# The first units of a scan in front of an FFN: dummies out, two steps moved, one load split

## The chip, the cores and the metric

One core of one Trainium2 chip runs the program. The time is device microseconds of one execution, and the median of several runs is compared. The engines are TensorE (PE, with its weight loads PEld), VectorE (DVE), ScalarE (ACT), GpSimd (POOL) and SyncE (SP), which only issues DMAs; ScalarE issues one DMA too. Each engine takes its own instructions in the order in which they are written, and waits at an instruction for what that one needs.

## The reference

Two parts. The first is a chunked scan with decays, for 4 batches, 8 heads, 768 steps, head size 32 and state size 16:

```python
log_a = np.log(np.clip(a, 1e-06, 1.0))
for c in range(nc):                       # chunks of the sequence
    cum = np.cumsum(la, axis=-1)
    L = np.exp(cum[:, :, :, None] - cum[:, :, None, :]) * causal
    M = np.einsum('bhin,bhjn->bhij', Cc, Bc) * L
    y_intra = np.einsum('bhij,bhjd->bhid', M, xc)
    y_inter = np.einsum('bhin,bhnd->bhid', Cc, state) * np.exp(cum)[:, :, :, None]
    y[:, :, sl] = y_intra + y_inter
    Bx = np.einsum('bhjn,bhjd->bhjnd', Bc, xc) * np.exp(cum[:, :, -1:] - cum)[:, :, :, None, None]
    state = np.exp(np.sum(la, axis=-1))[:, :, None, None] * state + np.sum(Bx, axis=2)
```

The second is an FFN over the 3072 tokens of 256 channels that the scan gives: `h = x @ w_in` (256 to 2048), `g = max(0.01 * h, h)`, `g @ w_out` (2048 to 256). The FFN weights come as 64-bit floats and are turned into pairs of 32-bit floats on the chip.

## The kernel before

The scan uses chunks of 96 steps instead of 32: 8 chunks times 4 batches are 32 units, and a unit holds the 8 heads of one batch and chunk. For each unit the kernel needs four things.

- **Decays**: the exponent of every pair of steps, made by TensorE into a two-bank buffer `pd`, and an exponential by ScalarE into the tile `lt` (decay_of, L276). Units 0 and 1 do it directly from `la` (decay_mask L239, decay_direct L246). Later units take one product of two tiles `dl` and `dr` (decay_pe, L265). Parts of these hold the running sums, which VectorE splits in three (split_sums, L227 to L230), SyncE writes to DRAM (`parts_d`, L618), and DMAs read back into `dl` (L254) and `dr` (L257). For the first two of these slots the DMA of `dr` is issued by ScalarE.
- **Scores**: products of C and B in two halves (L321), each half in a score buffer of its own; VectorE multiplies them into `lt` (L326).
- **Products**: `lt` with x (L348), and the decayed B with x for the state (L357), into a `pd` buffer.
- **Outputs** (unit_halves): ScalarE copies the state part (`stage`, L381) and rounds the output (`xh`, L386), GpSimd writes the state into the next chunk's x (L384), and `rest()` takes on VectorE what the rounding lost (`xl`, L391).

The decayed B is made once per chunk: the column product (columns, L217) on TensorE, an exponential `erev` on ScalarE (L218), a multiplication on GpSimd (state_decay, L303).

The order is written out by hand: what is called first stands first on every engine that it uses. Two pools of buffers tie the engines together. `ps_c` has two score buffers (score_tile): `first`, with the row sums, and `second`, with the column product in its first bank, are the two at the start, and the two halves of unit 0's scores take the same two again. `ps_d` has two buffers too (free_tile): units 0 and 1's decays take one each, then they alternate, so that the products of a unit take one and the decays of the unit two ahead the other. In the loop over the first ten units the decays of unit u + 2, the scores of unit u + 1 and the products of unit u follow each other; for u = 0 the products come first, so that unit 2's decays take the buffer of unit 1's, and unit 3's decays the buffer of unit 0's products.

keep_warm (L128) issues dummy products on a zero tile, whose results nobody reads: six at the start, two behind the decay masks, two in unit 0 and one ahead of the scores of units 2, 3 and 4. Weight blocks (`raw`, 512 KB each, fetch_w at L100) are decoded by ScalarE (L445) and VectorE (L452 to L472) among the units. Behind the ten units the FFN runs in 54 and more steps on TensorE, with the remaining units between them.

Of the kernel before, what the change touches and what calls it, by code (L numbers as in the profile page):

```python
# [10 lines left out]
F32 = mybir.dt.float32  # L11
# [7 lines left out]
Q = 96  # L19
# [41 lines left out]
BUSY = (17, 21, 25, 30, 34, 38, 42, 46, 50)  # L61
LIGHT = (9, 11, 13, 14, 16)
KD = Q + 3 * NH + 3
MAG_MIN = float(np.uint32(0x38000000).view(np.float32))
MAG_MAX = float(np.uint32(0x47EFFFFF).view(np.float32))

# [2 lines left out]
def scan_ffn(ctx: ExitStack, tc: tile.TileContext, a_l, b_l, c_l, bn_l, x_l, w_l, out_l):  # L69
# [25 lines left out]

    raws, bcs, xss, bns = {}, {}, {}, {}

    def fetch_w(f, eng=nc.sync):
        raws[f] = wr.tile([128, 2 * DM, 2], U32, name="raw")
        eng.dma_start(raws[f].rearrange("p c w -> p (c w)"), w_l[f].bitcast(U32))  # L100

    ccs = [pst.tile([128, 2, NB, Q], F32, name=f"cc{i}") for i in range(2)]

# [22 lines left out]
    def keep_warm(space, n):  # L126
        for _ in range(n):
            nc.tensor.matmul(  # L128
                space.rearrange("p (a b) -> p a b", b=128), lhsT=idle,
                rhs=idle.unsqueeze(1).to_broadcast([128, 4, 128]), start=True, stop=True,  # L130
            )
# [50 lines left out]
    def fill_first():  # L182
        nc.vector.tensor_copy(dr[:Q, 0], later.unsqueeze(1).to_broadcast([Q, NH, Q]))

    def fill_less():
        rows = slice(Q, Q + 3 * NH)
        nc.scalar.copy(dr[rows, 0], less[rows].unsqueeze(2).to_broadcast([3 * NH, NH, Q]))
# [15 lines left out]
        )  # L203

    nc.vector.tensor_copy(upto_b, upto)

    erev = const.tile([QE, ncols], F32, name="erev")
    ccol = const.tile([QE, ncols], F32, name="ccol")
# [100 lines left out]

    def scores(u, warm=0):
        c, b = divmod(u, NB)
        lt = lts[u].rearrange("p (g h) i -> p g (h i)", h=2)
        for half in range(2):
            sc = score_tile()
            if half == 0 and warm:
                keep_warm(sc[:, 0], warm)
            for g in range(2):
                r = 32 * (2 * half + g)  # L320
                nc.tensor.matmul(  # L321
                    sc[:QE, g, :2 * Q].rearrange("p (k i) -> p k i", k=2), lhsT=bcs[c][r:r + 32, b * QE:(b + 1) * QE],
                    rhs=ccs[c % 2][r:r + 32, :, b], start=True, stop=True,
                )
            heads = lt[:, 2 * half:2 * half + 2]
            nc.vector.tensor_tensor(out=heads, in0=sc[:QE, :, :2 * Q], in1=heads, op=ALU.mult)  # L326
# [270 lines left out]
    with tc.tile_pool(name="ps_d", bufs=2, space=PSUM, reuse_waits="tile") as ps_d:  # L597
# [9 lines left out]
        second = score_tile()  # L607
        for u in range(DIRECT):
            fill_reach(u)
        nc.gpsimd.memset(ccs[1], 0.0)  # L610
        nc.vector.memset(dl[Q:], 1.0)
        nc.vector.memset(dl[Q:Q + 3 * NH, :, Q:], 0.0)
        fill_first()
        fill_less()
        prow = first[:, 0, :Q]
        sum_rows(prow, 0)
        split_sums(prow)
        nc.sync.dma_start(parts_d, parts)  # L618
        fetch_w(0)
        for u in range(DIRECT):  # L620
            decay_mask(pds[u])
        keep_warm(second[:, 1], WARM2)
        columns(erev, after, AF.Exp, second[:, 0])
        state_decay(0)
        decay_direct(0, pds[0])
        decay_of(0, pds[0])
        fill_slots(1, SLOTS // 2)
        scores(0)
        decay_direct(1, pds[1])
        nc.scalar.copy(dl[:Q], upto_b.unsqueeze(1).to_broadcast([Q, SLOTS, QE]))  # L630
        decay_load(DIRECT, 2, nc.scalar)
        decay_load(DIRECT + 2, SLOTS - 2)
        decay_of(1, pds[1])
        fill_slots(SLOTS // 2, SLOTS)
# [3 lines left out]
        for u in range(FIRST_UNITS):  # L638
            v = u + 2
            if u:  # L640
                decay_pe(v, free_tile())
            if u == 0:
                rest = unit_out(u, free_tile())
                rest()
            if u + 1 < FIRST_UNITS:
                scores(u + 1, int(0 < u < 4))
            else:
                pair_now((), (u + 1, u + 2))
                settle()
                state_decay(3)  # L650
                abs_more()
                pg = ctx.enter_context(tc.tile_pool(name="pg", bufs=LAG + 2))
                ffn_in(0, free_tile()[:, 0])
            if u:
                rest = unit_out(u, free_tile())
                rest()
            else:
                pd = free_tile()
                keep_warm(pd[:, 0], WARM2)
                decay_pe(v, pd)  # L660
            c, b = divmod(u, NB)
            if u == 1:
                fetch_w(1)
            if c + 2 <= 3:
                if b == 2:
                    fetch_bc(c + 2)
                if b == 3:
                    fetch_bn(c + 2)
            if u == 3:
                fetch_x(2)  # L670
            if u == 5:
                fetch_w(2)
            if u == 7:
                alloc_x(3)
                fetch_x(3)
            if u > 7:
                fetch_more()
            if u in (2, 5):
                state_decay(1 if u == 2 else 2)
            if u:  # L680
                settle()
            if u == 1:
                decode_abs(0)
            if u == 4:
                decode_abs(1)
            decode(LEAD.get(u, 0))
# [326 lines left out]
```

## Time and profile before

| | |
|---|---|
| median of 3 runs | 318.17 us (317.96 to 318.62) |
| profiled execution | 318.41 us, its span 316.7 us |
| busy: PE, DVE, ACT, POOL | 310.4, 212.0, 180.7, 128.5 us |
| first FFN product | at 29.24 us |
| median time of the 512 KB weight loads, issue to landing | 3.3 us |

Times in rows are microseconds from the start of the span. A row of the timeline gives start, length, engine, line, operation, what is written from what, how many instructions were merged, and in brackets how long the engine was idle before and what ended that. PE's lengths reach to the end of the pipeline, so that rows of PE overlap; the distance from one start to the next is what an instruction takes of its queue. A q behind an engine's name is its queue, which issues DMAs.

### The profile page before, as it was taken

What the parts mean: (1) busy time and instruction counts of PE and PEld (TensorE: products, weight loads), DVE (VectorE), ACT (ScalarE), POOL (GpSimd) and SP (SyncE); (2) the same over time, 40 slices, a digit from 0 to 9 for tenths busy, and PEclk for the clock granted to TensorE, in tenths of its full rate; (3) what the DMA queues carried; (4) which work ended last, traced back from release to release, by engine and by line L of the source; (5) the groups of instructions that cost most, each with busy time, mean ns of one, the idle gap of its engine ahead of it and who ended that gap; (6) DMA issues with size and microseconds to landing.
All of it is one profiled execution on the core that took longest, in us unless ns stands there. A gap on an engine that the chain in (4) does not pass through costs nothing.

```text
span 316.7 us, 6261 instructions
## 1 busy us (share of the span) xinstructions
PE 310.4 (98%) x2407; PEld 245.8 (78%) x2407; DVE 212.0 (67%) x350; ACT 180.7 (57%) x353; POOL 128.5 (41%) x215
## 2 busy tenths in 40 slices
PE   8999999999999999999999999999999999999995
PEld 4566877777888878888887878788887888888884
DVE  5697787898987677767634444277367676767561
ACT  3776776848574755646454634375365547645551
POOL 6288644614554242724434330070035466335100
PEclk9999999999999999999999999999999999999999
DMA  6987626094518322350204101000001000000003
GB/s 166 253 223 232 173 81 214 23 274 133 155 67 248 108 89 66 96 126 2 90 0 156 66 1 68 0 2 0 0 0 66 2 0 0 2 0 0 2 2 132
DMA packets 11722, 26.29 MB, mean 83 GB/s; under 512 B 2380, under 2 KB 4652, under 8 KB 11692
## 3 DMA queue, kind: packets, MB, share of 16 engines
q1 hardware_dynamic: 11641, 25.88, 27.3%
q8 instruction: 19, 0.31, 0.4%
q14 instruction: 11, 0.09, 0.1%
q10 hardware_dynamic: 51, 0.01, 0.0%
HBM read 22.57 MB, written 3.32 MB: 82 GB/s over the span
## 4 chain that ended last, share of the span: by engine, by line
PE 95%; DVE 2%; ACT 1%; issue 1%; DVEq 0%; ACTq 0%
PE op L578 27%; PE hp L554 26%; PE sc L800 9%; PE op L820 7%; PE sc L820 6%; PE hp L800 3%; PE sc L411 3%; PE sc L348 3%; PE sc L321 2%; PE pd L348 1%; PE pd L265 1%; PE sc L128 1%; PE pd L246 1%; DVE w L465 1%; PE sc L357 1%
## 5 line engine op out<-in xcount | busy, mean ns | idle before, releaser
L567 DVE TENSOR_TENSOR gl<-hp,gh 128x512 fp32r<-128x512 f32 x63 | 43.4, 689 | 55.4 <-ACT hp L564 55.3
L561 ACT ACTIVATE gh<-hp 128x512 fp32r<-128x512 f32 x63 | 37.6, 598 | 63.0 <-PE hp L554 62.9
L578 PE MATMUL op<-gh,wh 128*128 128x512 f32 x128 | 50.9, 398 | 0.0
L554 PE MATMUL hp<-xh,wh 128*128 128x512 f32 x126 | 50.0, 397 | 0.4 <-DVE gl L567 0.4
L578 PE MATMUL op<-gh,wl 128*128 128x512 f32 x128 | 49.9, 390 | 0.0
L578 PE MATMUL op<-gl,wh 128*128 128x512 f32 x128 | 49.8, 389 | 0.0
L554 PE MATMUL hp<-xl,wh 128*128 128x512 f32 x126 | 49.2, 390 | 0.0
L554 PE MATMUL hp<-xh,wl 128*128 128x512 f32 x126 | 49.2, 390 | 0.0
L384 POOL COPY xs<-stage 16x64 f32<-16x64 f32 x112 | 30.8, 275 | 30.5 <-ACT stage L381 25.9
L766 POOL TENSOR_TENSOR sl<-s,sh 128x512 fp32r<-128x512 f32 x8 | 10.4, 1295 | 71.3 <-ACT sh L765 71.3
L564 ACT ACTIVATE hp<-hp 128x512 f32<-128x512 f32 x63 | 37.5, 595 | 0.0
L297 POOL TENSOR_SCALAR_AFFINE_SELECT lt<-lt 96x768 f32<-96x768 f32 x16 | 15.7, 982 | 47.8 <-ACT lt L296 47.8
L288 POOL TENSOR_TENSOR lt<-lt,ccol 112x768 f32<-112x768 f32 x16 | 25.2, 1577 | 10.8 <-DMA lt<-crow_d 6.0
L578 PEld LDWEIGHTS op<-gh,wh 128*128 128x128 f32 x128 | 24.0, 188 | 7.0 <-issue 1.4
L554 PEld LDWEIGHTS hp<-xh,wh 128*128 128x128 f32 x126 | 23.7, 188 | 5.9 <-DVE gl L567 0.8
L578 PEld LDWEIGHTS op<-gl,wh 128*128 128x128 f32 x128 | 24.0, 188 | 5.1
L554 PEld LDWEIGHTS hp<-xl,wh 128*128 128x128 f32 x126 | 23.6, 188 | 5.4 <-DVE xl L391 0.5
L578 PEld LDWEIGHTS op<-gh,wl 128*128 128x128 f32 x128 | 24.0, 188 | 4.6
L554 PEld LDWEIGHTS hp<-xh,wl 128*128 128x128 f32 x126 | 23.7, 188 | 4.8 <-DVE wl L485 0.2
L424 DVE TENSOR_TENSOR lt<-sc,lt 112x384 f32<-112x384 f32 x44 | 21.6, 548 | 3.5 <-ACT xh L386 1.8
L833 DVE TENSOR_TENSOR gl<-c,gh 128x512 fp32r<-128x512 f32 x24 | 23.1, 962 | 1.0 <-ACT c L830 0.7
L829 ACT ACTIVATE gh<-hp 128x512 fp32r<-128x512 f32 x8 | 4.8, 600 | 27.2 <-PE hp L800 27.2
(164 smaller groups left out, 617.0 us busy)
## 6 DMA issues: line engine op xcount, KB each, us to landing
raw<-w_l SPq DMA_DIRECT2D x16, 512.0 KB, 3.3
lt<-crow_d SPq DMA_DIRECT2D x16, 336.0 KB, 4.6
xs<-x_l SPq DMA_DIRECT2D x8, 384.0 KB, 8.2
out_l<-ob SPq DMA_DIRECT2D x12, 256.0 KB, 2.2
bn<-bn_l SPq DMA_DIRECT2D x8, 231.0 KB, 3.8
bt<-b_l SPq DMA_DIRECT2D x8, 224.0 KB, 6.4
cc<-c_l SPq DMA_DIRECT2D x16, 96.0 KB, 4.6
la<-a_l SPq DMA_DIRECT2D x1, 96.0 KB
```

Of the source, the lines that this page charges most:

```text
L288: nc.gpsimd.tensor_tensor(out=lts[u], in0=lts[u], in1=ccol[:, u * NH:(u + 1) * NH].unsqueeze(2).to_broadcast([QE, NH, Q]), op=ALU.subtract,)
L297: nc.gpsimd.affine_select(out=lt[:Q], in_=lt[:Q], pattern=[[0, NH], [1, Q]], compare_op=ALU.is_ge, fill=0.0, base=0, channel_multiplier=-1,)
L384: nc.gpsimd.tensor_copy(to[:, :, hh], stage[hh * D:hh * D + N])
L424: nc.vector.tensor_tensor(out=heads, in0=spaces[half][:QE, :, 2 * Q * e:2 * Q * (e + 1)], in1=heads, op=ALU.mult,)
L554: nc.tensor.matmul(hp, lhsT=w_half[half][:, f, k * 128:(k + 1) * 128], rhs=x[t][:, k, :], start=(n == 0), stop=(n == 5),)
L561: nc.scalar.activation(ghs[s], hp, AF.Prelu, alpha=0.01)
L564: nc.scalar.activation(hps[s], hps[s], AF.Prelu, alpha=0.01)
L567: nc.vector.tensor_tensor(out=gls[s], in0=hps.pop(s), in1=ghs[s], op=ALU.subtract)
L578: nc.tensor.matmul(op, lhsT=w_half[half][:, f, DM + m * 128:DM + (m + 1) * 128], rhs=x, start=(first and i == 0), stop=(last and i == 2),)
L800: nc.tensor.matmul(bank, lhsT=w[h], rhs=x[g], start=start and i == 0, stop=i == 2, skip_group_check=True,)
L820: nc.tensor.matmul(outs[t][m], lhsT=w_half[half][:, f, DM + m * 128:DM + (m + 1) * 128], rhs=x, start=first and i == 0, stop=last and i == 2,)
L833: nc.vector.tensor_tensor(out=gl, in0=g, in1=gh, op=ALU.subtract)
```

## The change

Seven edits, all ahead of the FFN:

- The dummies of the units go: the two in unit 0, and the one ahead of the scores of units 2, 3 and 4. Those at the start and behind the masks stay.
- The column product, `erev` and the multiplication of B go behind unit 0's direct decays and their exponential.
- The ones in `dl` are set on VectorE ahead of the clipping of `la`, as 32-bit words that hold two ones each.
- ScalarE fills `dl` right behind fill_less, and issues its DMA of `dr` ahead of unit 0's exponential.
- The memset of the second `cc` buffer on GpSimd goes behind the multiplication of B.
- Weight block 0 is loaded in two halves; between them stands the first DMA of `dl`.
- In unit 0, `rest()` goes behind the scores of unit 1.

```diff
-    def fetch_w(f, eng=nc.sync):
-        raws[f] = wr.tile([128, 2 * DM, 2], U32, name="raw")
-        eng.dma_start(raws[f].rearrange("p c w -> p (c w)"), w_l[f].bitcast(U32))
+    def fetch_w(f, half=None):
+        if f not in raws:
+            raws[f] = wr.tile([128, 2 * DM, 2], U32, name="raw")
+        part = slice(0, 2 * DM) if half is None else slice(half * DM, (half + 1) * DM)
+        nc.sync.dma_start(
+            raws[f][:, part].rearrange("p c w -> p (c w)"),
+            w_l[f].bitcast(U32).rearrange("p (c w) -> p c w", w=2)[:, part].rearrange(
+                "p c w -> p (c w)"
+            ),
+        )
...
     nc.vector.tensor_copy(upto_b, upto)
+    nc.vector.memset(dl[Q:].rearrange("p b j -> p (b j)").bitcast(F32), ONES)
...
-    def scores(u, warm=0):
+    def scores(u):
...
             sc = score_tile()
-            if half == 0 and warm:
-                keep_warm(sc[:, 0], warm)
...
             fill_reach(u)
-        nc.gpsimd.memset(ccs[1], 0.0)
-        nc.vector.memset(dl[Q:], 1.0)
+        fill_first()
         nc.vector.memset(dl[Q:Q + 3 * NH, :, Q:], 0.0)
-        fill_first()
         fill_less()
+        nc.scalar.copy(dl[:Q], upto_b.unsqueeze(1).to_broadcast([Q, SLOTS, QE]))
         prow = first[:, 0, :Q]
         sum_rows(prow, 0)
         split_sums(prow)
         nc.sync.dma_start(parts_d, parts)
-        fetch_w(0)
+        fetch_w(0, 0)
         for u in range(DIRECT):
             decay_mask(pds[u])
         keep_warm(second[:, 1], WARM2)
+        fill_slots(1, SLOTS // 2)
+        decay_direct(0, pds[0])
+        decay_load(DIRECT, 2, nc.scalar)
+        decay_of(0, pds[0])
         columns(erev, after, AF.Exp, second[:, 0])
         state_decay(0)
-        decay_direct(0, pds[0])
-        decay_of(0, pds[0])
-        fill_slots(1, SLOTS // 2)
+        nc.gpsimd.memset(ccs[1], 0.0)
         scores(0)
         decay_direct(1, pds[1])
-        nc.scalar.copy(dl[:Q], upto_b.unsqueeze(1).to_broadcast([Q, SLOTS, QE]))
-        decay_load(DIRECT, 2, nc.scalar)
+        fetch_w(0, 1)
         decay_load(DIRECT + 2, SLOTS - 2)
...
             if u == 0:
                 rest = unit_out(u, free_tile())
-                rest()
             if u + 1 < FIRST_UNITS:
-                scores(u + 1, int(0 < u < 4))
+                scores(u + 1)
...
-                pd = free_tile()
-                keep_warm(pd[:, 0], WARM2)
-                decay_pe(v, pd)
+                rest()
+                decay_pe(v, free_tile())
```

How the instructions stand is shown here at three places; line numbers of the changed program are five to nine higher for the same line.

First ScalarE, from the fill of `dr` to unit 1's exponential; `lt` from `pd` is the exponential of a unit's decays, `erev` that of the column product. Before:

```order
L187 COPY dr<-less 24x768
L218 ACTIVATE erev<-sc 112x256
L276 ACTIVATE lt<-pd 112x768
L630 COPY dl<-upto_b 96x896
L257 DMA dr<-parts_d 3x16x96
L276 ACTIVATE lt<-pd 112x768
```

Changed:

```order
L195 COPY dr<-less 24x768
L620 COPY dl<-upto_b 96x896
L266 DMA dr<-parts_d 3x16x96
L285 ACTIVATE lt<-pd 112x768
L227 ACTIVATE erev<-sc 112x256
L285 ACTIVATE lt<-pd 112x768
```

The copy and the DMA moved ahead of unit 0's exponential, and `erev` moved behind it.

Then TensorE, from the column product (`sc` from `la` and `after`) to unit 2's and 3's decays (`pd` from `dr` and `dl`). Before:

```order
L217 MATMUL sc<-la,after 112x256
L246 MATMUL pd<-lt,after 112x384 x2
L321 MATMUL sc<-cc_95,bt 112x192 x4
L246 MATMUL pd<-lt,after 112x384 x2
L348 MATMUL pd<-lt,xs 32x96 x8
L357 MATMUL pd<-xs,bn 32x32 x8
L321 MATMUL sc<-cc_95,bt 112x192 x4
L128 LDWEIGHTS idle
L128 MATMUL pd<-idle 128x512
L128 LDWEIGHTS idle
L128 MATMUL pd<-idle 128x512
L265 LDWEIGHTS dl
```

Changed:

```order
L255 MATMUL pd<-lt,after 112x384 x2
L226 MATMUL sc<-la,after 112x256
L328 MATMUL sc<-cc_95,bt 112x192 x4
L255 MATMUL pd<-lt,after 112x384 x2
L355 MATMUL pd<-lt,xs 32x96 x8
L364 MATMUL pd<-xs,bn 32x32 x8
L328 MATMUL sc<-cc_95,bt 112x192 x4
L274 LDWEIGHTS dl
```

The column product now stands between unit 0's decays and unit 0's scores, and the dummies are gone.

Last VectorE, from the fill of the first `dr` slots to the multiplications of unit 2. Before:

```order
L191 COPY dr<-dr 120x2304
L326 TENSOR_TENSOR lt<-sc,lt 112x384 x2
L191 COPY dr<-dr 120x3072
L391 TENSOR_TENSOR xl<-pd,xh 128x2x96
L326 TENSOR_TENSOR lt<-sc,lt 112x384 x4
```

Changed:

```order
L199 COPY dr<-dr 120x2304
L333 TENSOR_TENSOR lt<-sc,lt 112x384 x2
L199 COPY dr<-dr 120x3072
L333 TENSOR_TENSOR lt<-sc,lt 112x384 x2
L398 TENSOR_TENSOR xl<-pd,xh 128x2x96
L333 TENSOR_TENSOR lt<-sc,lt 112x384 x2
```

The two multiplications of unit 1 now stand ahead of `xl` of unit 0.

More of the change, by code (lines that the diff above doesn't have):

```diff
@@ L63 @@
 KD = Q + 3 * NH + 3
+ONES = float(np.uint32(0x3F803F80).view(np.float32))
 MAG_MIN = float(np.uint32(0x38000000).view(np.float32))
```

## The prediction

> **What bounds the kernel now.** I read the page first, then the chain of waits, then each engine's timeline from 3 to 20 us, where every edit lies.
>
> ```profile
> span 316.7 us, 6261 instructions
> PE 95%; DVE 2%; ACT 1%; issue 1%; DVEq 0%; ACTq 0%
> 11.24 0.54 PE pd L128 x2
> 12.47 0.22 PE sc L128
> 14.31 0.22 PE sc L128
> 16.15 0.22 PE sc L128
> ```
>
> The chain is TensorE's in 95% of the span, and the five dummies that the change takes out of the units lie on it with 0.54 + 3 x 0.22 = 1.20 us. Read no further and that is the gain. But a chain that follows a pipelined engine says little of what that engine waits for, so the stretch itself decides.
>
> ```profile
> 16.00:20.00 4.00, 4.00 (x88) 2.40 (x86) 3.96 (x10) 2.62 (x8) 3.56 (x9) 1.00 0.77 207
> 20.00:24.00 4.00, 3.95 (x89) 2.70 (x88) 3.96 (x12) 3.72 (x11) 3.50 (x10) 1.00 0.85 232
> ```
>
> In these rows of the windows (stretch, length, then busy time of PE, PEld, DVE, ACT and POOL) VectorE has 3.96 of 4.00 us. From 16 us on a unit cannot go faster than VectorE lets it, whatever TensorE saves. Only what moves VectorE's work of unit 3 (L326 at 15.15) reaches the end, and it reaches it whole: behind the units TensorE runs the FFN without slack.
>
> **The column product goes behind unit 0's decays.** Unit 0 now, with every engine that takes part:
>
> ```profile
> 3.34 0.81 DVE L611 MEMSET dl<- 32x896 bf16 x1 [0.24 <-issue]
> 3.69 0.71 PE L221 MATMUL sc<-upto,la 96*128 96x96 f32 x2
> 4.37 0.36 DVE L183 COPY dr<-later 96x768 bf16<-96x768 bf16 x1
> 4.64 0.25 DVE L227 CAST parts<-sc 128x96 bf16<-128x96 f32 x1
> ...
> 6.24 0.60 PE L217 MATMUL sc<-la,after 96*112 96x256 f32 x2
> 6.68 1.45 PE L246 MATMUL pd<-lt,after 96*112 96x384 f32 x4
> 6.88 0.38 ACT L218 ACTIVATE erev<-sc 112x256 f32<-112x256 f32 x1 [2.47 <-PE sc L217]
> 7.34 1.06 POOL L303 TENSOR_TENSOR bn<-bn,erev 112x512 f32<-112x512 f32 x1 [1.15 <-ACT erev L218]
> 7.78 0.75 SPq L254 DMA_DIRECT2D dl<-parts_d  x2
> 8.06 0.59 PE L321 MATMUL sc<-cc,bt 32*112 32x192 f32 x8
> 8.16 0.81 ACT L276 ACTIVATE lt<-pd 112x768 f32<-112x768 f32 x1 [0.91 <-PE pd L246]
> 8.23 0.51 ACTq L257 DMA_DIRECT2D dr<-parts_d  x1
> 8.58 1.54 PE L246 MATMUL pd<-lt,after 96*112 96x384 f32 x4
> ...
> SPq L254 <- DMA parts_d<-parts: 1.0, 1, 1.0
> ```
>
> TensorE runs column product, unit 0's decays, unit 0's scores and unit 1's decays back to back. With the two first exchanged, the decays start at 6.24 instead of 6.68 and end at 6.24 + 1.45 = 7.69; the scores still come at 8.06. The exponential lt of unit 0 could start at 7.72 instead of 8.16, a gain of 0.44.
>
> On ScalarE, though, the DMA of dr now stands ahead of that exponential, and it needs parts_d in DRAM. Today it stands behind it and its wait costs nothing. The memset of 0.81 leaves VectorE's way, so the cast L227 waits only for the row sums (3.69 + 0.71 = 4.40, say 4.45 instead of 4.64), and everything up to parts_d comes 0.2 sooner: landed at about 7.78 - 0.2 = 7.6. The last row, of the waits, shows what such a wait does: SyncE's queue stands still 1.0 us at L254 for parts_d, the DMAs behind it too. ScalarE's will do the same, and issuing takes 0.51, so lt starts at 8.1. The gain of 0.44 shrinks to 0.05.
>
> The Trainium skill ("DMA: Bandwidth & Descriptors", Anatomy of one DMA) says that a semaphore wait of a DMA is taken by the issuing sequencer before dispatch; by that lt stands still until 8.1. By the row at 8.23 alone, an issue beside a running exponential, lt might pass at 7.72, and the stall below would be 0.4 shorter.
>
> Then the price. The column product is written into the second score buffer. There are two such buffers, and the second half of unit 0's scores takes that one again, so it must wait until the exponential erev (L218) has read it. Today erev is done at 7.26, 0.8 before. In the new order erev stands behind lt on ScalarE: from the next two rows ScalarE goes from one lt to the next instruction in 10.87 - 10.16 = 0.71.
>
> ```profile
> 10.06 0.54 PE L348 MATMUL pd<-lt,xs 96*32 96x96 f32 x16
> 10.16 0.81 ACT L276 ACTIVATE lt<-pd 112x768 f32<-112x768 f32 x1 [0.23 <-PE pd L246]
> 10.65 0.59 PE L321 MATMUL sc<-cc,bt 32*112 32x192 f32 x8
> 10.87 0.20 ACT L381 COPY stage<-pd 128x64 f32<-128x64 f32 x1
> ```
>
> So erev runs 8.1 + 0.71 = 8.81 to 9.19, and the second half of the scores starts at 9.25. Scores take 8.58 - 8.06 = 0.52 of TensorE's queue, a half 0.26, and unit 1's decays, queued behind, start at 9.51 instead of 8.58: **+0.93**. TensorE has nothing else: all of unit 0's products stand behind them. Bounds: if the DMA wait does not hold ScalarE, lt at 7.72 gives +0.55; if parts_d comes no sooner, 7.78 + 0.51 gives lt at 8.29 and +1.12. I take 0.93, since a waiting DMA held its queue in the row of L254.
>
> From those decays to the products is 8.06 - 6.68 = 1.38 where nothing intervenes; today it is 10.06 - 8.58 = 1.48, as the products also wait for VectorE. So products at 10.89, **-0.10** of the stall given back, and scores of unit 1 at 10.89 + 0.59 = 11.48 (today 10.65, +0.83). The decayed B (L303, 1.06) follows erev and is ready at 9.25 + 1.06 = 10.3, ahead of its use at 11.2.
>
> **The rest of unit 0's halves (xl) goes behind unit 1's scores.** The rows of units 1 to 4:
>
> ```profile
> 11.33 0.36 DVE L391 TENSOR_TENSOR xl<-pd,xh 128x192 fp32r<-128x192 f32 x1 [0.43 <-PE sc L321]
> 11.61 1.01 DVE L326 TENSOR_TENSOR lt<-sc,lt 112x384 f32<-112x384 f32 x2
> 13.32 1.02 DVE L326 TENSOR_TENSOR lt<-sc,lt 112x384 f32<-112x384 f32 x2 [0.70 <-PE sc L321]
> 15.15 1.02 DVE L326 TENSOR_TENSOR lt<-sc,lt 112x384 f32<-112x384 f32 x2 [0.41 <-PE sc L321]
> 17.25 1.02 DVE L326 TENSOR_TENSOR lt<-sc,lt 112x384 f32<-112x384 f32 x2
> ...
> 11.66 0.81 PE L265 MATMUL pd<-dr,dl 123*112 123x384 bf16 x4
> 12.62 0.64 PE L321 MATMUL sc<-cc,bt 32*112 32x192 f32 x8
> 13.18 0.54 PE L348 MATMUL pd<-lt,xs 96*32 96x96 f32 x16
> 13.80 0.50 PE L265 MATMUL pd<-dr,dl 123*112 123x384 bf16 x2
> 14.46 0.59 PE L321 MATMUL sc<-cc,bt 32*112 32x192 f32 x8
> 17.42 0.53 PE L265 MATMUL pd<-dr,dl 123*112 123x384 bf16 x2
> 17.88 1.02 PE L321 MATMUL sc<-cc,bt 32*112 32x192 f32 x8
> ```
>
> Unit 3's decays (the second pair of the x4 at 11.66, so about 11.66 + 0.81 - 0.50 = 11.97) reuse the buffer from which xl of unit 0 is read. xl now stands behind both multiplications of unit 1, which start 0.70 after the scores (13.32 - 12.62) and take 1.02. So multiplications at 11.48 + 0.70 = 12.18, xl at 13.2 to 13.56, unit 3's decays at 13.6, +1.63. Scores follow such a pair after 17.88 - 17.42 = 0.46, today after 12.62 - 11.97 = 0.65 with a dummy between: unit 2's scores at 14.06 instead of 12.62, **+1.44**. So xl behind adds 1.44 - 0.83 = **+0.61**. Three dummies are out of it already: unit 0's two would lie under the wait for xl, the third is the 0.65 against 0.46. Bounds: +0.3, if the multiplications start on the first half of the scores; +0.8, if 1.06 lies between them and xl.
>
> **The other dummies.** From unit 2's scores the products of unit 1 and the next pair of decays follow as today (13.18 and 13.80). The dummy behind them is worth (14.46 - 13.80) - 0.46 = **-0.20**; the last lies ahead of unit 4's scores, whose multiplication at 17.25 waits for VectorE's own queue: nothing. Unit 3's multiplications come at 15.15 + 1.44 - 0.20 = 16.39, +1.24, and VectorE, full from there, carries it to the FFN. Bounds: -0.1 to -0.6, if all of them counted.
>
> **Edits that cost nothing.** The ones memset, half as many elements as the one of 0.81, goes into the time in which VectorE waits for la (without that cover la, and all behind it, would be late by up to 0.4); dl's fill by ScalarE lies between its 4.41 and the DMA wait; both fills are long done. The weights' first block comes in two halves, both issued by about 8.7; ScalarE reads it behind unit 1's outputs, past 15. cc's memset moves behind the decayed B, so chunk 1's loads are issued up to 2 us later, at 11.2:
>
> ```profile
> DMA to landing us min/median/max: 2.4/3.5/4.6
> ```
>
> By this row of cc its second part lands by 11.2 + 0.6 + 4.6 = 16.4, and unit 4's scores come at 17.5; that cover of 1.1 us gone, unit 4 would be late by what lacks.
>
> **Sum:** +0.93 - 0.10 + 0.61 - 0.20 = +1.24. Ends: 0.55 - 0.10 + 0.3 - 0.6 = +0.15 and 1.12 + 0.8 - 0.1 = +1.8. The profiled execution took 318.41 (span 316.7, and 1.7 around it), which gives 319.65; it is 0.24 above the median of the runs, so I forecast **319.4** by the median 318.17.
>
> **Rivals.**
> - *Faster, TensorE's chain as it reads.* If TensorE's own issue sets the pace in the units, the five dummies give their 1.20: 317.0. For it speaks the chain; against it the two rows of windows, and that two of the moved steps are waits that TensorE gets. It decides if erev is done before 8.1. Chance 0.08.
> - *Half the stall.* The queue of ScalarE lets lt pass, or xl costs nothing, or a later wait swallows part: +0.2 to +0.6, 318.6. For it: each of the two terms rests on one wait that today's trace does not show. Against it: both buffers have no third, and the order on ScalarE and VectorE is fixed. Chance 0.16.
> - *The clock falls.* Without dummies and with two stalls of about 1 us TensorE's clock could fall. A dummy costs 0.22 in the chain at 12.47, and at the start:
>
> ```profile
> 1.06 2.74 PE L128 MATMUL sc<-idle 128*128 128x512 bf16 x6 [1.06 <-DVE idle L124]
> ```
>
> That is 0.46 each, so half speed. Two units of 1.6 us at half speed give +3.2 more: 322.6. Against it: in units 4 to 9 no dummy stands, and the pair at 17.42 takes 0.53 as the one at 13.80 takes 0.50. Chance 0.05. The Trainium skill ("TensorE: Matmul & The Clock Gate", What's actually happening) asks for an idle window of some 3.4 us before the clock is halved; by that the chance would be smaller still.
> - The forecast has 0.71.
>
> **How the numbers follow.** The likeliest case spans +0.7 to +1.8 about 319.4. The range takes in the half stall: the ends of the sum, +0.15 and +1.8, with the spread of the runs shown, 0.21 below their median and 0.45 above, are 318.1 and 320.4. A measurement here tells 0.2%, 0.64 us, from no change: slower than 318.81 is nearly all of the forecast, a quarter of the half stall and the clock, 0.66 + 0.04 + 0.05 = 0.75; faster than 317.53 is 0.08 and a little, 0.09; within it 0.16.
>
> **What would show it.** In the new profile: the DMA of dr issued on ScalarE at about 7.6 with lt behind it at 8.1; erev near 8.8; a gap on TensorE before the second half of unit 0's scores, ended by erev; unit 1's decays at 9.5; unit 3's decays waiting for xl at 13.6; unit 3's multiplications near 16.4. Wrong, if unit 1's decays start before 9.0 or unit 3's multiplications before 15.6: then the waits are not those, and TensorE's chain was right.

## The result, and the profile after

The changed kernel took 319.9 us, the median of six executions (319.41 to 325.72), beside 317.92 for the kernel before, of six as well: a ratio of 1.0063, 95% interval 1.0042 to 1.0085. Two of the six, 324.78 and 325.72, ran at a mean granted clock of 0.972 and 0.974 and are not in the ratio. The profiled execution took 319.75 against 318.41 before, spans 318.0 and 316.7.

First ScalarE and SyncE in the changed kernel, from their timelines (start, duration, engine, line, operation; in brackets the idle time ahead and what ended it):

```profile
5.64 0.35 SPq L624 DMA_DIRECT2D parts_d<-parts  x1
7.90 0.37 SPq L263 DMA_DIRECT2D dl<-parts_d  x1
7.90 0.50 ACTq L266 DMA_DIRECT2D dr<-parts_d  x1
8.45 0.81 ACT L285 ACTIVATE lt<-pd 112x768 f32<-112x768 f32 x1 [3.15 <-PE sc L226]
9.16 0.38 ACT L227 ACTIVATE erev<-sc 112x256 f32<-112x256 f32 x1
```

Both queues go on at 7.90: that is the landing of the sums (parts_d). The exponential of unit 0 follows ScalarE's load at 8.45, and erev follows the exponential. The bracket at 8.45 names TensorE's column product as the last semaphore, although TensorE had the decays done at about 7.55 (6.09 + 1.46); what held ScalarE is the load in front, as the row above it shows. Then TensorE:

```profile
6.09 1.46 PE L255 MATMUL pd<-lt,after 96*112 96x384 f32 x4
7.91 0.58 PE L328 MATMUL sc<-cc,bt 32*112 32x192 f32 x4
9.59 0.58 PE L328 MATMUL sc<-cc,bt 32*112 32x192 f32 x4 [1.10 <-ACT erev L227]
10.10 1.54 PE L255 MATMUL pd<-lt,after 96*112 96x384 f32 x4
11.57 0.54 PE L355 MATMUL pd<-lt,xs 96*32 96x96 f32 x16
12.16 0.59 PE L328 MATMUL sc<-cc,bt 32*112 32x192 f32 x8
14.20 0.48 PE L274 MATMUL pd<-dr,dl 123*112 123x384 bf16 x2 [0.98 <-DVE xl L398]
14.61 0.59 PE L328 MATMUL sc<-cc,bt 32*112 32x192 f32 x8
16.19 0.78 PE L328 MATMUL sc<-cc,bt 32*112 32x192 f32 x8
30.52 0.50 PE L561 MATMUL pd<-xh,wh 128*128 128x512 f32 x1
```

Unit 0's scores are cut in two, with a wait of 1.10 for erev between the halves, and unit 3's decays wait 0.98 for xl. These are the two waits that the prediction named. The FFN starts at 30.52. From TensorE's timeline of the kernel before, two rows: a stall in unit 7's products, and the FFN's start.

```profile
25.29 0.44 PE L348 MATMUL pd<-lt,xs 112*32 112x96 f32 x10 [0.32 <-issue]
29.24 0.50 PE L554 MATMUL pd<-xh,wh 128*128 128x512 f32 x1
```

From the FFN's start to the end both spans have 287.5 us (318.0 - 30.52 and 316.7 - 29.24): between these two, nothing is gained or lost behind the units. VectorE in the changed kernel:

```profile
12.86 1.02 DVE L333 TENSOR_TENSOR lt<-sc,lt 112x384 f32<-112x384 f32 x2 [0.70 <-PE sc L328]
13.80 0.35 DVE L398 TENSOR_TENSOR xl<-pd,xh 128x192 fp32r<-128x192 f32 x1
16.89 1.02 DVE L333 TENSOR_TENSOR lt<-sc,lt 112x384 f32<-112x384 f32 x2 [0.19 <-PE sc L328]
19.17 1.01 DVE L333 TENSOR_TENSOR lt<-sc,lt 112x384 f32<-112x384 f32 x2
```

The first two rows are unit 1's multiplications and unit 0's xl. Unit 3's multiplications stand at 16.89 (15.15 before), unit 4's at 19.17 (17.25 before). The chain of waits is TensorE's in 85% of the span where it was 95%, but that share says little of the change: it is 84% where only the dummies are gone, and 93% with B, defined below, undone.

### The profile page after: what moved, and what is told of

It reads as the page before. It is cut to its first block, busy times and chain, and to the rows that moved or that the text cites. A ratio compares the mean times of both kernels' runs of the same rounds, so it can differ in the third digit from the quotient of the medians.

```text
span 318.0 us, 6255 instructions
## 1 busy us (share of the span) xinstructions
PE 310.0 (97%) x2402; PEld 245.7 (77%) x2402; DVE 212.8 (67%) x350; ACT 180.5 (57%) x353; POOL 128.4 (40%) x215
## 4 chain that ended last, share of the span: by engine, by line
PE 85%; DVE 4%; POOL 4%; issue 2%; ACT 2%; DMA 1%; ACTq 0%; DVEq 0%; POOLq 0%
PE op L585 26%; PE hp L561 25%; PE sc L805 9%; PE op L825 7%; PE sc L825 6%; PE hp L805 3%; POOL xs L391 3%; PE sc L418 3%; PE sc L355 3%; DVE w L472 1%; PE sc L136 1%; POOL wl L520 1%; ACT lt L285 1%; DMA parts_d<-parts 1%; PE sc L364 1%
```

## The experiments

Each was timed in interleaved rounds with the kernel before; ratios are to that. A is the move of the column product, with erev and the multiplication of the tensor B, behind unit 0's decays; B is the move of unit 0's `rest()`. The load of dr ahead of unit 0's exponential is a third move, and belongs to neither. For the first four the kernel before took 317.61.

**A undone.**

```diff
+        columns(erev, after, AF.Exp, second[:, 0])
+        state_decay(0)
         decay_direct(0, pds[0])
         decay_load(DIRECT, 2, nc.scalar)
         decay_of(0, pds[0])
-        columns(erev, after, AF.Exp, second[:, 0])
-        state_decay(0)
```

> The changed kernel with one edit undone: the column product, erev and the multiplication of B stand ahead of unit 0's decays again. Theory of the two waits: the stall of 1.1 us before the second half of unit 0's scores goes; the DMA still holds unit 0's exponential until about 8.4, so the products of unit 0 start at about 10.3 (before 10.06, changed 11.57); xl still stands behind unit 1's multiplications, so unit 3's decays at about 13.0 and unit 3's multiplications at about 15.6 to 15.7 (before 15.15, changed 16.89). Time: 1.1 to 1.4 us below the changed kernel, 0.4 to 0.7 above before. Rival, the missing dummies (TensorE's clock or its chain): unit 3's multiplications stay near 16.9 and the time within 0.3 us of the changed kernel's.

Measured: 318.61, ratio 1.0027 (1.0013 to 1.0042). Its timelines:

```profile
8.16 0.51 ACTq L266 DMA_DIRECT2D dr<-parts_d  x1
8.72 0.81 ACT L285 ACTIVATE lt<-pd 112x768 f32<-112x768 f32 x1 [1.47 <-PE sc L328]
...
8.57 1.54 PE L255 MATMUL pd<-lt,after 96*112 96x384 f32 x4
10.18 0.84 PE L355 MATMUL pd<-lt,xs 96*32 96x96 f32 x16
11.07 0.59 PE L328 MATMUL sc<-cc,bt 32*112 32x192 f32 x8
```

The wait for erev is gone, unit 1's decays are back at 8.57 (8.58 before the change), and 1.1 of the 2.0 us come back (0.0036 of 318; the two intervals just touch). The load, still in front, now holds the exponential itself to 8.72, so unit 1's scores stay 0.42 behind those of the kernel before (10.65). B's wait is untouched (0.98 ahead of unit 3's decays, at 13.10).

**B undone.**

```diff
             if u == 0:
                 rest = unit_out(u, free_tile())
+                rest()
...
             else:
-                rest()
                 decay_pe(v, free_tile())
```

> The changed kernel with one edit undone: xl of unit 0 stands ahead of unit 1's scores again. Theory of the two waits: the stall by erev stays, unit 1's decays at 10.1; unit 3's decays at about 13.3 instead of 14.20, but unit 1's multiplications move from 12.86 to about 13.1, so unit 2's multiplications gain only 0.4 to 0.5 (about 14.85 instead of 15.31). Time: 0.3 to 0.6 us below the changed kernel, about 1.4 above before. Rival, that the wait for xl is hidden by the other: no difference, within 0.2.

Measured: 319.99, ratio 1.0068 (1.0051 to 1.0084): nothing came back. TensorE's timeline, and VectorE's row of unit 3's multiplications:

```profile
12.68 1.05 PE L274 MATMUL pd<-dr,dl 123*112 123x384 bf16 x4
13.72 1.05 PE L328 MATMUL sc<-cc,bt 32*112 32x192 f32 x8
...
27.43 0.37 PE L355 MATMUL pd<-lt,xs 112*32 112x96 f32 x8 [1.12 <-issue]
...
16.45 1.02 DVE L333 TENSOR_TENSOR lt<-sc,lt 112x384 f32<-112x384 f32 x2 [0.19 <-PE sc L328]
```

The wait for xl is gone and unit 2's scores come 0.89 sooner (13.72 against 14.61), unit 3's multiplications 0.44 (16.45 against 16.89). But in unit 7's products TensorE stood 1.12 us with nothing to wait for that the profile shows, and the FFN starts at 31.27, later than in the change. TensorE's instructions are the same and in the same order in both. So the wait is what the prediction said it is; that its end is worth time was not shown by this run. The profiled execution, 320.78, was also the longest of the five in the ratio (the others 319.19 to 320.02), so its stall does not by itself say why the other four gained nothing.

**A and B undone**, the two edits above together.

> Both edits undone; what stays of the change is the dummies out, the ones and ScalarE's fill sooner, the DMA of dr ahead of unit 0's exponential, block 0 in two parts, cc's memset behind the multiplication of B. Theory of the two waits: no gap of TensorE by erev or xl; unit 0's exponential at about 8.4 (before 8.16), which costs about 0.25, the dummy ahead of unit 3's scores gives 0.2 back: within 0.3 us of before. Rival, the missing dummies cost the time: near the changed kernel, 1.5 us or more above before. Rival, TensorE's chain: 1.2 below before.

Measured: 318.22, ratio 1.0017 (1.0006 to 1.0028). The timelines of ScalarE and TensorE show what is left:

```profile
8.46 1.51 ACT L285 ACTIVATE lt<-pd 112x768 f32<-112x768 f32 x2 [2.23 <-DMA parts_d<-parts]
...
5.64 1.45 PE L255 MATMUL pd<-lt,after 96*112 96x384 f32 x4
9.92 0.83 PE L355 MATMUL pd<-lt,xs 96*32 96x96 f32 x15 [0.82 <-DVE lt L333]
```

In this execution TensorE was a microsecond early (direct decays at 5.64; the section on the hardware has a likely reason), ready before 7.1, and ScalarE still started the exponential only at 8.46, behind the load that had waited for the sums; TensorE then stood 0.82 ahead of unit 0's products, for VectorE's multiplications behind that exponential.

**The dummies alone:** the kernel before, with its five dummies taken out and nothing else.

```diff
-                scores(u + 1, int(0 < u < 4))
+                scores(u + 1)
...
-                pd = free_tile()
-                keep_warm(pd[:, 0], WARM2)
-                decay_pe(v, pd)
+                decay_pe(v, free_tile())
```

> The kernel before with only the five dummies of the units taken out. Theory of the two waits and of VectorE as the pace from 16 us: 0.1 to 0.4 us faster, unit 3's multiplications at about 14.9 instead of 15.15. Rival, TensorE's chain as the view of it reads: 1.2 us faster. Rival, the clock: slower, with a granted clock below 0.99 or dummies at the start alone not enough.

Measured: 317.27, ratio 0.9988 (0.9976 to 0.9999), so 0.3 to 0.4 us. The 1.20 us that the chain of waits had for them were not there to be won: the interval reaches 0.8 us at most. TensorE's row of unit 2's and unit 3's decays, ahead of which the two dummies of unit 0 had stood:

```profile
10.80 0.83 PE L265 MATMUL pd<-dr,dl 123*112 123x384 bf16 x4 [0.65 <-DMA dl<-parts_d]
```

In their place TensorE waits 0.65 for dl, more than the 0.54 that the two had in the chain. In this profile unit 3's multiplications stand 8.49 behind the start of the direct decays (14.07 - 5.58), where they stood 8.47 before (15.15 - 6.68). Its direct decays start 1.1 sooner, so the load comes late for it; up to there it shows no gain by the dummies, and what took it is a load, not VectorE.

For the next four the kernel before took 318.0.

**The load of dr behind unit 0's exponential**, A and B as in the change.

```diff
-        decay_load(DIRECT, 2, nc.scalar)
         decay_of(0, pds[0])
+        decay_load(DIRECT, 2, nc.scalar)
         columns(erev, after, AF.Exp, second[:, 0])
```

> The change as it is, but ScalarE issues the load of dr behind the exponential of unit 0's decays instead of ahead of it; the column product, the later rest() and all else stay. Theory (the load takes the semaphore wait for the sums' landing, so the decays behind it cannot start before 7.90 us): that exponential starts at about 7.5 us (the end of the direct decays' matmuls, as before with TensorE's work 0.6 us nearer) instead of 8.45, erev at about 8.3 instead of 9.16, the waiting half of the scores at about 8.7 instead of 9.59, unit 1's decays at 9.2 instead of 10.10: 0.9 us sooner in the units; of that 0.6 to 0.9 in the time, so about 319.2 where the kernel before has 317.6 and the change itself 319.9 (ratio to before 1.003 to 1.005). Rival (the wait is for TensorE or VectorE, the load in front costs nothing): unit 1's decays stay at 10.1 and the ratio at 1.006 to 1.007.

Measured: ratio 1.0057 (1.0037 to 1.0076), no gain that can be told from the change's 1.0063. In its profile the granted clock is 0.50 for a good part of the units (the last section shows it), so the rows are taken from a second measurement of the same kernel:

> The load of dr behind the exponential of unit 0's decays once more, for a profile at full clock, since in the one taken the granted clock was 0.50 from 10.5 to 34 us. Theory (the load in front holds the exponential): unit 1's decays 0.7 to 0.9 us sooner after the direct decays' start than in the change (4.01 us after it there), and the time's missing gain is to be seen behind them, as a stall or a queue that the change did not have. Rival (with TensorE late, the exponential waits for it rather than for the load): unit 1's decays 3.7 to 4.0 us after the direct decays' start, and nothing is gained in the units either.

Measured: 319.45 (before 317.93), ratio 1.0052 (1.0033 to 1.0071).

```profile
7.22 0.81 ACT L285 ACTIVATE lt<-pd 112x768 f32<-112x768 f32 x1 [1.92 <-PE pd L255]
7.89 0.51 ACTq L266 DMA_DIRECT2D dr<-parts_d  x1
8.44 0.38 ACT L227 ACTIVATE erev<-sc 112x256 f32<-112x256 f32 x1 [0.41 <-PE sc L328]
...
5.73 1.45 PE L255 MATMUL pd<-lt,after 96*112 96x384 f32 x4
9.39 1.54 PE L255 MATMUL pd<-lt,after 96*112 96x384 f32 x4
```

These are ScalarE and TensorE. The exponential is free and starts 1.49 after the direct decays, but the load, now between it and erev, holds erev instead. Unit 1's decays stand 3.66 after the direct decays' start (9.39 - 5.73) where the change has 4.01. My expectation of 0.7 to 0.9 had looked at the instruction behind the load and not at the next one. That count makes the gain look small, though: in both kernels the decays follow a load that waits for the landing of the sums, at 7.89 and 7.90, and that did not move with the direct decays (5.73 and 6.09). From the start of the span they come 0.71 sooner (9.39 against 10.10), and the FFN as much (29.80 against 30.52); in the span 0.4 is left, as a stall of 0.22 in the products behind the first FFN products grows to 0.46. The last run puts the load behind both (before 318.04):

```diff
-        decay_load(DIRECT, 2, nc.scalar)
         decay_of(0, pds[0])
         columns(erev, after, AF.Exp, second[:, 0])
+        decay_load(DIRECT, 2, nc.scalar)
         state_decay(0)
```

> The change as it is, but ScalarE issues the load of dr behind both unit 0's exponential and erev's; when it stood between the two, its wait for the sums (until 7.89 us) and its 0.5 us held erev to 8.44 instead. Counted from the start of unit 0's direct decays on TensorE. Theory (two things hold the second half of unit 0's scores: erev standing behind an exponential of 0.71, and the load of dr in front of both): the exponential at +1.5, erev at +2.35 where the change has +3.07 and the load between has +2.71, the second half at +2.8, unit 1's decays at +3.3 (change +4.01, load between +3.66); no wait for the sums on ScalarE's path, and 0.4 to 0.7 us less time than the change, ratio 1.0035 to 1.005; the load itself lands 0.4 to 0.7 us later, which unit 2's decays at +6.2 do not wait for. Rival (the load's place is immaterial, and the small difference seen so far was the start of the execution): unit 1's decays at +3.6 or later, ratio 1.005 to 1.007.

Measured: 318.98, ratio 1.0028 (1.0008 to 1.0049).

```profile
8.69 0.38 ACT L227 ACTIVATE erev<-sc 112x256 f32<-112x256 f32 x1
...
6.32 1.63 PE L255 MATMUL pd<-lt,after 96*112 96x384 f32 x4
9.12 0.58 PE L328 MATMUL sc<-cc,bt 32*112 32x192 f32 x4 [0.23 <-ACT erev L227]
9.63 1.54 PE L255 MATMUL pd<-lt,after 96*112 96x384 f32 x4
```

Counted from the direct decays' start, erev is at +2.37, the half at +2.80, unit 1's decays at +3.31: each as the theory had it, and the wait on TensorE falls from 1.10 to 0.23. The ratio falls by 0.0035 from the change's, 1.1 us where 0.4 to 0.7 was expected, and as much as by moving the column product back; the intervals are too wide to tell the two apart, and this one overlaps the change's a little. The profiled execution, 319.77, is not among the faster ones and shows no gain in its time.

**Everything back, with the load behind the exponential:** A and B undone and the load moved, so that only the missing dummies, the early fills, the later clearing of the C buffer and the split load of block 0 are left.

> The column product back ahead of the direct decays, rest() back at unit 0's products, and the load of dr behind the exponential of unit 0's decays: of the change there stay the missing dummies, the ones set early, ScalarE's fill of dl sooner, the clearing of the second C buffer later and block 0's load in two parts. Theory (the three moves are all of the loss): as the kernel before without its dummies, 317.3 us, ratio 0.998 to 1.0005; the exponential of unit 0's decays waits for TensorE alone, and unit 1's decays stand where they stood before. Rival (the rest of the change costs 0.3 us or more, by the split load or by the fill): ratio 1.001 to 1.002, as in the run with both moves undone and the load still ahead (1.0017).

Measured: 317.46, ratio 0.9993 (0.9975 to 1.0012). Against the run with A and B undone (1.0017) only the load's place differs: 0.0024, some 0.8 us, though the intervals overlap a little.

```profile
7.07 0.81 ACT L285 ACTIVATE lt<-pd 112x768 f32<-112x768 f32 x1 [0.91 <-PE pd L255]
...
5.58 1.45 PE L255 MATMUL pd<-lt,after 96*112 96x384 f32 x4
8.96 0.54 PE L355 MATMUL pd<-lt,xs 96*32 96x96 f32 x16
```

Unit 0's products come 3.38 after the start of the direct decays instead of 4.28 (9.92 - 5.64). The waits for the sums and for erev are gone from the path, and the rest of the change costs nothing that was measured.

**Chunk 0's x loaded behind the store of the sums**, all else as in the change.

```diff
     fetch_bn(0)
-    fetch_x(0)
...
         nc.sync.dma_start(parts_d, parts)
+        fetch_x(0)
         fetch_w(0, 0)
```

> The change as it is, but chunk 0's x is loaded behind the store of the sums instead of ahead of it (its 384 KB are read first by unit 0's products at 11.57 us). Theory (the store's landing is held by the x load's bytes in the same queues: 7.82 us with an issue at 5.64, where the estimate of the prediction was 7.6): SyncE's wait for the store ends at 7.5 to 7.6 instead of 7.90, the exponential of unit 0's decays starts at 8.1 instead of 8.45, and unit 1's decays at 9.75 instead of 10.10; the products do not wait for x, and the time falls by 0.2 to 0.35 us against the change (ratio to before about 1.005). Rival (the store takes 2.2 us by itself, whatever runs beside it): the wait still ends at 7.85 to 7.95 and nothing moves; if x lands behind 11.5 us, the products wait for it instead.

Measured: 319.56, ratio 1.0056 (1.0037 to 1.0075).

```profile
5.66 0.34 SPq L623 DMA_DIRECT2D parts_d<-parts  x1
7.33 0.51 ACTq L265 DMA_DIRECT2D dr<-parts_d  x1
```

With the same issue time (5.66 against 5.64) the store is done at 7.33 instead of 7.90: SyncE's wait ended together with ScalarE's. So the x load ahead of it had held it for 0.57 us. The other profiles bear it out: from issue to that wait's end the store takes 1.67 here and 1.61 in the next kernel, where x is behind it too, and 1.94 to 2.52 in all those with x ahead. The time's gain, 0.2 us by ratio, is too small to be told from nothing.

**x and block 0's weights behind the small loads, in the kernel without dummies.**

```diff
-    fetch_x(0)
...
         nc.sync.dma_start(parts_d, parts)
-        fetch_w(0)
+        fetch_x(0)
...
         decay_load(DIRECT + 2, SLOTS - 2)
+        fetch_w(0)
```

> The kernel before without its five dummies (317.27 us, ratio 0.9988), and in it the load of chunk 0's x behind the store of the sums and block 0's weights behind both loads of the decay rows. In the run without the dummies unit 2's decays waited 0.65 us for dl at 10.80. Theory (these loads lie behind the 384 KB of x and the 512 KB of weights): dl lands 0.4 to 0.9 us sooner, that wait is gone, and the time is 0.3 to 0.6 us under the run without the dummies, so a ratio of 0.997 to 0.9985. Rival (the small loads' own time decides, or VectorE, which is full from 16 us, takes the gain): ratio 0.9985 to 1.000. Unit 0's products, ready at about 9.0 us, wait for x if it lands later than that, which would cost up to 0.5 us.

Measured: 318.87, ratio 1.0037 (1.0017 to 1.0057), slower by 0.005 than the same kernel with the loads in their old places. TensorE's timeline has the two places:

```profile
9.98 0.54 PE L347 MATMUL pd<-lt,xs 96*32 96x96 f32 x16 [0.33 <-DMA xs<-x_l]
11.77 0.83 PE L264 MATMUL pd<-dr,dl 123*112 123x384 bf16 x4 [0.60 <-DMA dr<-parts_d]
```

Unit 0's products wait for x, as the expectation allowed, and the decay rows come no sooner. x had been in the way of the sums' store; that behind it x is in the way of their loads is likely and was not shown by itself. The theory on the weights, that moving them too would bring the rows sooner, fell. Counted from the direct decays, unit 3's multiplications come 0.35 later than without the move (8.84 against 8.49), so the rest of the 1.6 us lies elsewhere; the profile has stalls of 0.38 and 0.32 put down to issue in the units.

For the last two kernels, and the second measurement above, the kernel before took 317.93.

**A's wait filled:** unit 1's direct decays stand on TensorE between the two halves of unit 0's scores.

```diff
         for half in range(2):
+            if half and between:
+                between()
             sc = score_tile()
...
-        scores(0)
-        decay_direct(1, pds[1])
+        scores(0, lambda: decay_direct(1, pds[1]))
```

> The change as it is, but the direct decays of unit 1 (four matmuls, 1.46 us) stand on TensorE between the two halves of unit 0's scores, where the change leaves TensorE waiting for erev. Theory (A costs what TensorE stands idle there): the second half comes at about 9.65 instead of 9.59 and waits for nothing, unit 0's products at 10.7 to 10.9 instead of 11.57, unit 1's scores at 11.4 instead of 12.16; 0.6 to 0.9 us of the change's 1.9 comes back, 318.9 to 319.3 (ratio 1.003 to 1.0045), if what follows does not give it away. And if that idle time is also what lets the clock fall in some executions, none lies above 322. Rival (the column product's place costs through ScalarE's and VectorE's order, not through TensorE's idle time): products and scores stay within 0.2 us of where they were, ratio 1.005 to 1.007.

Measured: 319.49, ratio 1.0071 (1.0033 to 1.0108); one execution, 323.84, was above 322.

```profile
9.73 0.58 PE L330 MATMUL sc<-cc,bt 32*112 32x192 f32 x4
10.97 0.37 PE L357 MATMUL pd<-lt,xs 96*32 96x96 f32 x8 [0.36 <-DVE lt L335]
11.39 0.59 PE L330 MATMUL sc<-cc,bt 32*112 32x192 f32 x8
```

The half follows unit 1's decays and waits for nothing; the products now wait 0.36 for VectorE, and unit 1's scores come 5.47 after the direct decays' start (5.92) where the change has 6.07: 0.6 sooner. The ratio is too wide to say what this is worth, and the guess on executions above 322 was wrong.

**The same with B undone too.**

> As the run with the wait filled, and rest() of unit 0 back at its products (B undone): both named stalls gone with the column product still behind unit 0's decays. Theory (the two stalls are the loss, and they add): unit 3's decays follow unit 2's at once, scores(2) another 0.9 us sooner, unit 3's multiplications at 15.2 to 15.6 where the change has 16.89 and the kernel before 15.15; the time between 317.4 and 318.4, ratio 0.999 to 1.0025. Rival (undoing B gives nothing in the time, as it gave nothing beside the column product's move alone, since stalls of TensorE that the profile puts down to issue take it back): no faster than the run with the wait filled alone.

Measured: 318.66, ratio 1.0023 (1.0010 to 1.0037), 0.8 us below the run without it. TensorE's row for unit 3's decays:

```profile
12.43 0.49 PE L274 MATMUL pd<-dr,dl 123*112 123x384 bf16 x2 [0.17 <-DVE xl L400]
```

They wait 0.17 for xl instead of 0.98, and no stall put down to issue follows in the units. The direct decays start at 5.18 in this profile, so the half of unit 0's scores reaches its place sooner and again waits 0.49 for erev. So B does cost time, seen here where nothing behind takes the gain back; the rows of B alone show 0.44 of it.

Only one version is under the kernel before by more than its interval, and by little: without dummies it is 0.9988 (0.9976 to 0.9999).

## Why the prediction was right

The forecast was 319.4 and slower; measured were 319.9 and a ratio of 1.0063. The two waits were there, where and for the reasons that the prediction gave. The number was in part luck. In the terms in which the sum was made, 318.41 + 1.24 = 319.65 for a profiled execution, the profile has 319.75; but the terms came out as 1.52, 0, 0.48 and -0.26, together +1.74, and a stall that only the profile of the kernel before has hid the 0.5 by which the sum was short. Step by step:

- **"parts_d landed at 7.6, lt at 8.1": mis-sized.** The store was issued 0.20 sooner (5.64 against 5.84), as worked out, and yet landed at 7.90 against 7.78. The prediction took the landing to follow the issue. The run with x behind the store shows that x's load, ahead of it, set the landing, which the prediction had no term for. With 0.55 to issue the load, lt came at 8.45, 0.35 later than forecast; the upper bound, 8.29, had allowed for a landing no sooner, though not for one later.
- **That the load's wait stops ScalarE: right.** The exponential starts at 8.45 behind a load at 7.90, when its data was ready by 7.55, and erev was held to 8.44 when the load stood there. The Trainium skill ("DMA: Bandwidth & Descriptors", Anatomy of one DMA — SWDGE (gpsimd) path) has the issuing sequencer take a DMA's semaphore wait. The trace agrees, for a DMA that ScalarE issues.
- **erev 0.71 behind lt, the second half 0.44 behind that: right** (8.45, 9.16, 9.59).
- **A half of the scores as 0.26 of the queue: mis-sized.** The half that stands alone took 10.10 - 9.59 = 0.51, as long as both halves together (0.52 before). So unit 1's decays came 1.52 later instead of **+0.93**; 0.35 from lt and 0.25 from the half are the difference.
- **"-0.10" at the products: wrong.** 11.57 - 10.10 = 1.47, as before.
- **B "+0.61": nearly.** Unit 2's scores came at 14.61, 1.99 later than before, of which 1.51 stood already in unit 1's scores: +0.48. This is a net figure: beside the run with B undone B costs 0.89 at that place, and the dummies taken out there give 0.41 back. Of the 0.89, 0.44 reaches unit 3's multiplications.
- **The dummies "-0.20": about right.** Scores to scores is 1.58 (16.19 - 14.61) where it was 1.84 (14.46 - 12.62), so -0.26. The rival by which they give 1.20 fell in the run with the dummies alone, 0.3 to 0.4; in its profile a wait for dl took the place of the first two, which neither the rival nor the prediction had.
- **Unit 3's multiplications 16.4, carried by VectorE: the place was right, the time 0.5 short** (16.89, +1.74; unit 4's +1.92). To the FFN +1.28 was left, because the earlier profile has a stall in unit 7's products (25.29, issue): from their start to the next decays it takes 1.26 us, in the later one 0.59. That the place decides is borne out: in the eight profiles at full clock without such a stall in the units, the FFN starts 13.45 to 13.64 behind unit 3's multiplications.
- **The upper end, "+1.8", leaves out the -0.10** that the lower end has; with it, it is +1.72, just under the +1.74 that the units lost.
- **"0.24 above the median": wrong.** Between the medians lie 2.0 us, not 1.3. So by the medians the sum was short by 0.7. A reason that fits, but was not tested by itself, stands in the last section: some executions of the kernel before start up to 1 us sooner, and a kernel whose exponential waits for a store that lands at 7.9 can make no use of it.
- **The edits at nothing: right.** With A, B and the load undone the rest stands at 0.9993 (0.9975 to 1.0012), beside 0.9988 for the dummies alone.
- **The clock.** In the executions compared it did not fall; what was seen in others stands below.

## What to carry to other kernels

A load that waits for something stops its engine's queue, so look at every instruction behind it, not only the next one: here it held first the exponential, then erev, and only behind both did it hold neither. When two results share a buffer, moving the reader of the first behind other work holds the writer of the second: the column product, read late by erev's exponential, held the scores; unit 0's output, read late by xl, held unit 3's decays; and both waits appeared on TensorE, which was the bound. The chain of waits put 1.20 us on five dummies that were worth 0.3 to 0.4: what an engine would wait for once they are gone, in that run's profile a load, is not in the chain and has to be looked for in the timelines.

## What the runs showed of the hardware

**TensorE's first products run at two speeds, from one execution to another.** The same four mask matmuls, in the kernel before and in the run with everything back:

```profile
4.20 1.49 PE L239 MATMUL pd<-later,upto_b 96*112 96x384 bf16 x4
```

```profile
4.06 0.81 PE L248 MATMUL pd<-later,upto_b 96*112 96x384 bf16 x4
```

At nearly the same time they take 1.49 in one and 0.81 in the other, and the direct decays start at 6.68 or 5.58, though TensorE's work ahead is the same. The six dummies at the start take 0.46 each in the kernel before, the later ones 0.22, so a clock that is released sooner or later is the likely reason; the granted clock reads 1.00 in both profiles from the start and does not show it. Times are therefore mostly counted here from the direct decays, and not from the start of the span; where a wait ends with the landing of the sums, which does not move with TensorE (7.74 to 8.16 in the profiles with x ahead of the store, whose direct decays start between 5.02 and 6.68), that count misleads. The Trainium skill ("TensorE: Matmul & The Clock Gate", What's actually happening) says that the window that releases the clock runs free of the kernel's start; by that a spread between executions is expected, and these rows agree.

**The clock fell in some executions.** A row of TensorE's timeline and two of the windows, from the first profile of the kernel with the load behind the exponential (the windows' columns: stretch, length, busy time of PE, PEld, DVE, ACT and POOL, granted clock, DMA share, GB/s):

```profile
8.77 0.58 PE L328 MATMUL sc<-cc,bt 32*112 32x192 f32 x4 [1.35 <-ACT erev L227]
...
10.00:10.50 0.50, 0.50 (x3) 0.18 (x1) 0.50 (x1) 0.00 (x0) 0.50 (x1) 1.00 0.80 193
12.00:32.00 20.00, 19.38 (x268) 11.44 (x272) 12.32 (x28) 10.29 (x26) 10.20 (x27) 0.50 0.54 162
```

The clock is full up to 10.5 us and 0.50 from there to 34, with TensorE busy 19.38 of 20 us in the row shown, and that execution took 326.61. TensorE's longest wait just ahead was 1.35 us, for erev. A mean clock below 0.98 was seen in six executions, all of kernels with A (two of the change, three with the load behind the exponential, one with the wait filled), and in none without A; one without it, with x and the weights behind, had 0.982. The same section of the Trainium skill names an idle window of some 3.4 us as what halves the clock, and a busy one as what restores it. These rows show a fall without such an idle window, and some 23 us of work at half clock. The rival "the clock falls" had the effect, then, for some executions of the kernels with A; what starts it stays open, since the run with the wait filled had one too.

**TensorE stands still with nothing to wait for.** Stalls of 0.3 to 1.1 us that the profile puts down to issue came at unit 4's or unit 7's products (0.32 before, 1.12 with B undone, 0.38 with A and B undone, none in the change), also between kernels whose TensorE instructions and their order are the same (the change and B undone; A and B undone and everything back, which has none). In the profile with B undone one took back all that was gained. The products behind the first FFN products have another, 0.18 to 0.73; the profile puts some of these down to GpSimd's `wl`, though in two of them (0.46 and 0.73) its row ends 0.3 and 0.6 before the stall does.

The traces point to a cause. In the profile with x and the weights behind, all three places have a stall (19.47, 25.70 and 32.42), and from one to the next TensorE runs 126 matmuls and 125 or 126 weight loads. The records of DMA packets have 19 transfers of 16 KB of the kind "instruction" on a queue of their own; TensorE's 2402 matmuls and 2402 weight loads make 253 for each of them. All the stalls of this kind between 14 and 44 us, over all the profiles, end 1.2 to 1.6 us after one of these transfers ended: with B undone the transfer ended at 25.86 and the stall at 27.43. In the change it ended at 24.68, TensorE came to unit 7's products at 26.53, and did not stand. So TensorE most likely waits there for the next block of its own program. No run varied this, and what sets the start of those transfers is open.
